# Spacing attention scans inside spectral blocks: 3.0 slots for the first eight, 2.035 for the other forty, and PSUM banks lent from slot 10

## The chip, the core and the metric

The kernel runs on one core of one Trainium2 chip. A core has a matrix engine (TensorE: PE in the profile, with its weight loads listed apart as PEld), a vector engine (VectorE, DVE), a scalar engine (ScalarE, ACT), GpSimd (POOL), and SyncE (SP), which here only issues DMA transfers. Each engine runs its own instructions in the order in which they were written into its queue, and waits on semaphores for the others. Matrix products land in PSUM, which the program uses as eight banks of 128 x 512 float32.

The metric is the device time of one execution in microseconds (us), the median of three runs. Lower is better.

## What is computed

Two token mixers over 2048 tokens of width 512, joined by a gate:

```python
def _A_ref(x, wqkv, wo):            # attention, H = 32 heads of Dh = 16
    qkv = (x @ wqkv).reshape(B, S, 3, H, Dh).transpose(2, 0, 3, 1, 4)
    q, k, v = qkv[0], qkv[1], qkv[2]
    scores = jnp.einsum("bhqd,bhkd->bhqk", q, k) * scale
    p = _softmax(scores, axis=-1)
    o = jnp.einsum("bhqk,bhkd->bhqd", p, v)
    return o.transpose(0, 2, 1, 3).reshape(B, S, D) @ wo

def _B_ref(x, dft_seq_re, dft_seq_im, dft_hid_re, dft_hid_im):
    a = jnp.einsum("bsd,ed->bse", x, dft_hid_re)
    b = jnp.einsum("bsd,ed->bse", x, dft_hid_im)
    return jnp.einsum("ts,bse->bte", dft_seq_re, a) - jnp.einsum("ts,bse->bte", dft_seq_im, b)

g = _sigmoid((x * gate_w).sum(-1, keepdims=True))
return g * a + (1 - g) * b          # a, b: what the two return
```

## The kernel before

The program has four stages: projections (queries, keys, values and the two hidden-axis DFT products), the spectral stage (the sequence-axis DFT products), attention proper, and a last stretch in which attention runs beside the rest of the spectral work and the output projection. Float32 operands are split into a high and a low part in the format float32r, and a product is made of three: high x high, high x low, low x high.

**Scans.** Softmax subtracts a row maximum. The maxima are found in advance by *scans*: scan `n` computes a 128 x 512 piece of scores for the two heads of a pair and reduces it. Of the 1024 scans, the first 708 (`FRONT`) are put between other work ahead of attention. From scan 64 on they are folded (`scan_folded`, L160 to L181). Scan `n` has two halves, `j` = 0 and 1, for the two heads; each is one matmul (L174) with 64 contraction rows in its own half of the array, into its own PSUM bank. For even `c` ScalarE copies the result out (L178, `Relu`, tile `fold`); for odd `c` VectorE adds the new result to that tile and takes a maximum into `mx` (L180, one custom instruction and a short read of its accumulator). So scans alternate: one whose two banks ScalarE empties, then one whose two banks VectorE empties. The second half of scan `n` is issued together with the first half of scan `n+1` (`behind`).

**Slots.** All the product loops ahead of attention call `beside()` (L328 to L356) after each pair of product matmuls (`halves_of`, L201 to L205: two matmuls, one per half of the array, in two banks). One such call is a *slot*; `slots[0]` counts them. At each slot `beside` first runs what has fallen due (`after(n, f)` puts work `n` slots ahead: copies, splits, DMA issues), then adds `1 / pace[0]` to a credit and issues a scan when the credit reaches 1. `pace[0]` is thus a distance in slots: `PACE` 3.9, `SUMS` 5.2 and `BESIDE` 2.72 in the projections, `PART` 2.15 in most of the spectral stage, `SWAP` 2.97 while operands are exchanged in its middle.

**Blocks.** The spectral stage makes 22 *blocks* of 48 slots: 16 output row blocks `t` of phase 0 (`cr`, the cosine part), six of phase 1 (`ci`, the sine part). A block accumulates 96 product matmuls into the two banks of one *side*; sides alternate from block to block (`turns`, `xy`). Two blocks in each phase are made in halves (14 and 15 in phase 0, 0 and 1 in phase 1): that is where the operands are exchanged and `SWAP` holds. When a block is done, ScalarE scales its two banks into SBUF: `tx` at once (L771), `ty` five slots later (through `after`, so it has the line L318). GpSimd adds the two and SyncE stores the sum.

**Banks.** Four of the eight banks belong to the two sides. The other four, `d0`, `d1`, `k0`, `k1`, are the two *beds* of the scans (a bed is a bank for each half). A finished side is idle until the block after the next needs it, so it is lent as a third bed, `w`. `spare` holds the side and the slots between which it may be lent:

```python
if 0 < t < NB - 3 and n < len(coef) - NU - 1:      # L774, at a block's end
    spare[:] = side_of[t], slots[0] + 12, slots[0] + 44
...
side, since, until = spare                         # L296, in bed()
free = ["d", "k"] + ["w"] * (since <= slots[0] < until)
at = min(free, key=lambda a: places.get(a, -3))    # least recently used
```

So of the 48 slots of a block that follows a block with `0 < t < 13`, the first eleven and the last five have two beds and the rest have three. That holds for the twelve blocks `t` = 2 to 13 of phase 0 and for the three blocks `t` = 2 to 4 of phase 1, the fifteen blocks that the change reaches.

Of the kernel before, what the change touches and what calls it, by code (L numbers as in the profile page):

```python
# [37 lines left out]
FRONT = 564 + 16 * LATER - SAVED  # L38
FOLDED = range(SCANS, FRONT)
PACE, SUMS, BESIDE, PART, SWAP = 3.9, 5.2, 2.72, 2.15, 2.97  # L40
EARLY = [0, 4, 5, 6, 7, 1, 2, 3, 8, 9]
PARTS = {10: 20, 11: FRONT - SCANS * len(EARLY) - 20}
PART_PAIR, END_PAIR = PARTS
SEQ = [(p, i) for p in EARLY for i in range(SCANS)]
SEQ += [(p, i) for p, n in PARTS.items() for i in range(n)]
SEQ += [(p, i) for p in (PART_PAIR, 12, 13, 14, 15, END_PAIR) for i in range(PARTS.get(p, 0), SCANS)]
ROWS = {SCANS * n + (20 if n else 40): p for n, p in enumerate(EARLY[1:])}
ROWS.update({SCANS * len(EARLY) - 60: PART_PAIR, SCANS * len(EARLY) - 34: END_PAIR})
NWARM = 20
# [17 lines left out]
def build(tc, xT, wqkv, wo, wrT, wiT, cr, ci, ct, gate, out):  # L67
    nc = tc.nc
    with ExitStack() as ctx:
# [76 lines left out]
        def scan(n, ps):  # L146

            p, i = SEQ[n]
            qb, c = i // 4, i % 4
            qs, ks = scanned[p]  # L150
            if i == 0:
                new_maxima(p)
            for j in range(2):
                b = 64 * j
                nc.tensor.matmul(ps[:, j, :], qs[b:b + 48, qb * P:(qb + 1) * P],  # L155
                                 ks[b:b + 48, c * 512:(c + 1) * 512], start=True, stop=True)
            nc.vector.tensor_reduce(mx[p][:, :, qb, c], ps, axis=AX.X, op=ALU.max)  # L157
# [3 lines left out]
        def scan_folded(n, j, bank, pool):  # L161

            p, i = SEQ[n]
            qb, c = i // 4, i % 4
            if i == 0 and j == 0:
                new_maxima(p)
                if p in PARTS:  # L170
                    nc.vector.memset(mx[p], -3.0e38)
            qs, ks = scanned[p]
            b, ps = 64 * j, bank(n, j)
            nc.tensor.matmul(ps, qs[b:b + 64, qb * P:(qb + 1) * P], ks[b:b + 64, c * 512:(c + 1) * 512],  # L174
                             start=True, stop=True)
            if c % 2 == 0:
                fold[j] = pool.tile([P, 512], F32, tag=f"fold{j}", name="fold")
                nc.scalar.activation(fold[j], ps, AF.Relu)  # L178
            else:
                nc.vector.tensor_tensor_reduce(out=fold[j], in0=ps, in1=fold[j], scale=1.0, scalar=-3.0e38,  # L180
                                               op0=ALU.add, op1=ALU.max, accum_out=mx[p][:, j, qb, c // 2:c // 2 + 1])  # L181

        def shift(p, copy=nc.vector.tensor_copy, sub=nc.vector.tensor_sub):
# [9 lines left out]

            of = mx[p].rearrange("p j b c -> p (j b) c")[:, :, 0:2 if p in EARLY[1:] else 4]
            return [lambda: nc.vector.tensor_reduce(m, of, axis=AX.X, op=ALU.max, negate=True),
# [73 lines left out]
        seen, slots, due, count = [0], [0], [], [0]  # L269
        pace = [None, 0.0]  # L270
        with ExitStack() as pf:

            def s1():
                return pss1[0].tile([P, 2, 512], F32, tag="s1", name="s1")
# [3 lines left out]
            spare = [0, 0, 0]  # L278
# [31 lines left out]
            def run_due(force=(False, False)):  # L310

                while True:
                    ready = [d for d in due if d[0] <= slots[0] or force[d[2] in maxima]]
                    if not ready:
                        return
                    d = min(ready, key=lambda d: d[:2])
                    due.remove(d)
                    d[2](*d[3])  # L318

            def load_scan_beside(p):  # L320
                scanned[p], loads = row_loads(p, nc.sync, kf_d if p else k_d, p > 0)
                for n, load in enumerate(loads):
                    after(7 * n, load)
# [4 lines left out]
            def beside():  # L328

                slots[0] += 1  # L330
                run_due()
                if pace[0] is None:
                    return
                pace[1] += 1.0 / pace[0]
                while seen[0] < FRONT and pace[1] >= 1.0:
                    pace[1] -= 1.0
                    n = seen[0]
                    if n == FOLDED.start:
                        begin_folds()
                    if n in ROWS:  # L340
                        load_scan_beside(ROWS[n])
                    if n not in FOLDED:
                        scan(n, s1())
                        done = n
                    else:

                        scan_folded(n, 0, *beds)
                        done = behind(n - 1)
                    seen[0] += 1
                    if seen[0] == FRONT:  # L350
                        done = behind(n)
                    if done is not None and SEQ[done][1] == SCANS - 1:
                        for d, part in enumerate(shift(SEQ[done][0], nc.scalar.copy, nc.gpsimd.tensor_sub)):
                            maxima.append(part)
                            after((3, 8, 26, 31, 36)[d], part)
# [59 lines left out]
            def begin_folds():  # L415

                banks.close()
                psk.append(ctx.enter_context(tc.tile_pool(name="psk", bufs=1, space=PSUM, side="right", reuse_waits="tile")))
                beds.extend((bed, fp))
                scan_at(BESIDE)  # L420
# [255 lines left out]
            with ExitStack() as py:  # L676
# [11 lines left out]
                pss, yre, early, side_of = {}, {}, {}, {}  # L688
# [24 lines left out]
                for n, (ph, t, u) in enumerate(coef):  # L713
# [49 lines left out]
                    if u == NU - 1:  # L763
                        tx = cp.tile([P, D], F32, tag="tx", name="tx")
                        last = n == len(coef) - 1
                        ty = cp.tile([P, D], F32, tag="raw" if last else "ty", name="ty", bufs=5 if last else 2)
                        if last:
                            for v, ps in zip((tx, ty), pss[t]):
                                nc.vector.tensor_scalar_mul(v, ps, gm[:, t:t + 1])
                        else:  # L770
                            nc.scalar.mul(tx, pss[t][0], gm[:, t:t + 1])  # L771
                            if n == len(coef) - NU - 1:
                                nc.scalar.mul(ty, pss[t][1], gm[:, t:t + 1])
                            else:  # L774
                                after(5, nc.scalar.mul, ty, pss[t][1], gm[:, t:t + 1])
                        after(10, mixed, ph, t, yre.get(t), tx, ty)
                        if 0 < t < NB - 3 and n < len(coef) - NU - 1:
                            spare[:] = side_of[t], slots[0] + 12, slots[0] + 44
                run_due((True, True))

        assert seen[0] == FRONT + 1 and turns[0] % 2 == SCANS_IN, (seen, turns)
# [580 lines left out]
```

## Time and profile before

| | |
|---|---|
| median of three runs | 1711.61 us (1710.64 to 1711.81) |
| profiled execution, its own time | 1711.22 us |
| its span, first to last instruction | 1709.4 us |
| granted TensorE clock, mean | 0.999 |
| projections | 0 to 296.8 us |
| spectral stage | 296.8 to 658 us |
| attention, then attention beside the rest | 658 to 1258, 1258 to 1709 us |

Busy time in a view counts an engine as busy from an instruction's start to its end, and matmuls are pipelined: two run in the two halves of the array at once, and the next is taken in before the last is out. TensorE therefore shows nearly no idle time even where it loses time, and a loss is seen in two other ways: as more time for the same number of matmuls, and as idle time of the weight loader (PEld) that ends when ScalarE or VectorE has emptied a bank. In views of windows, "(x38)" counts the instructions that touch the window, so those that lie across its edges are in the count of both neighbours.

### The profile page before, as it was taken

To read this page: it belongs to the slowest core of one execution; us is meant where nothing else is said; L and a number is where in the kernel's file an instruction comes from. 1 tells how busy PE (TensorE), PEld (TensorE's weight loads), DVE (VectorE), ACT (ScalarE), POOL (GpSimd) and SP (SyncE) were. 2 spreads that over 40 slices of the span, in tenths; PEclk is the share of its full clock that TensorE was granted. 3 is DMA by queue.
4 is the path that set the end of the run, shared out by engine and by line. 5 is a ranking of instruction groups with operands and counts; after the bars stand their busy time and mean duration, and the time that the engine had idled before them with its cause. 6 is when DMAs were issued, how large, how long until landed. Compare 5 with 4: busy or idle time off the path is not lost.

```text
span 1709.4 us, 36306 instructions
## 1 busy us (share of the span) xinstructions
PE 1697.7 (99%) x13560; PEld 1022.3 (60%) x13560; DVE 1187.3 (69%) x2179; ACT 1491.7 (87%) x2472; POOL 764.3 (45%) x909
## 2 busy tenths in 40 slices
PE   9999999999999999999999999999999999999998
PEld 6888889989888885333333333333345555555554
DVE  5898888899999996666666666666642455654343
ACT  5447889888888888999999999999998888889876
POOL 3673435755555761434544455353423333334222
PEclk9999999999999999999999999999999999999999
DMA  7784557534348764356444445353436465576733
GB/s 253 246 284 106 155 167 230 172 117 121 115 121 219 197 135 95 97 133 138 136 114 111 122 121 134 95 131 78 100 69 145 136 151 146 142 164 163 194 92 127
DMA packets 149665, 246.73 MB, mean 144 GB/s; under 512 B 50048, under 2 KB 60784, under 8 KB 142192
## 3 DMA queue, kind: packets, MB, share of 16 engines
q1 hardware_dynamic: 134224, 223.04, 47.7%
q0 software_dynamic: 14688, 20.33, 4.9%
q8 instruction: 106, 1.74, 0.5%
q10 hardware_dynamic: 576, 1.05, 0.2%
q14 instruction: 71, 0.58, 0.1%
HBM read 164.10 MB, written 81.01 MB: 143 GB/s over the span
## 4 chain that ended last, share of the span: by engine, by line
PE 97%; DMA 1%; DVE 0%; issue 0%; ACT 0%; SPq 0%; DVEq 0%; ACTq 0%
PE pvb L808 29%; PE xy L205 26%; PE s L230 19%; PE s L174 9%; PE s L205 9%; PE s L155 5%; DMA q_d<-eh 0%; DMA raws<-wqkv 0%; DMA raws<-xT 0%; PE s L597 0%; DVE y L923 0%; DVE fold L180 0%; ACT fold L178 0%; SPq L567 0%; SPq L566 0%
## 5 line engine op out<-in xcount | busy, mean ns | idle before, releaser
L254 ACT ACTIVATE eb<-s 128x1024 f32<-128x1024 f32 x512 | 579.7, 1132 | 59.5 <-PE s L230 59.5
L262 ACT ACTIVATE e<-s 128x512 f32<-128x512 f32 x1022 | 609.4, 709 | 0.0
L157 DVE TENSOR_REDUCE mx<-s 128x2 f32<-128x1024 f32 x380 | 461.0, 1225 | 196.5 <-PE s L155 196.3
L808 PE MATMUL pvb<-eb,va 128*17 128x512 f32 x2052 | 514.4, 597 | 0.0
L808 PE MATMUL pvb<-e,va 128*17 128x512 f32 x2044 | 513.6, 597 | 0.0
L180 DVE CUSTOM_DVE_ANT_0 fold<-s,fold 128x512 f32<-128x512 f32 x644 | 432.5, 690 | 54.8 <-PE s L174 28.0
L178 ACT ACTIVATE fold<-s 128x512 f32<-128x512 f32 x644 | 376.8, 603 | 78.7 <-PE s L174 60.3
L230 PEld LDWEIGHTS s<-qs,ks 50*128 50x128 f32 x2048 | 214.0, 184 | 361.6 <-ACT eb L254 269.4
L230 PE MATMUL s<-qs,ks 50*128 50x512 f32 x2048 | 424.0, 435 | 0.0
L205 PE MATMUL xy<-b,c 64*128 64x512 f32 x2448 | 388.7, 391 | 0.1
L174 PE MATMUL s<-ks,qs 64*128 64x512 f32 x1288 | 319.2, 401 | 1.6 <-DVE mx L180 0.9
L205 PEld LDWEIGHTS xy<-b,c 64*128 64x128 f32 x2448 | 283.3, 184 | 28.4 <-issue 1.0
L174 PEld LDWEIGHTS s<-ks,qs 64*128 64x128 f32 x1288 | 173.9, 184 | 36.3 <-DVE mx L180 10.8
L808 PEld LDWEIGHTS pvb<-eb,va 128*17 128x17 f32 x2052 | 69.8, 96 | 189.3 <-issue 180.0
L155 PE MATMUL s<-ks,qs 48*128 48x512 f32 x760 | 153.4, 394 | 0.0
L205 PE MATMUL s<-b,b 64*128 64x512 f32 x1050 | 136.4, 391 | 0.0
L827 POOL DMA_DIRECT2D r_d<-lc x31 | 18.0, 580 | 260.3 <-DVE lc L826 212.7
L820 POOL DMA_DIRECT2D lc<-ob x124 | 63.1, 515 | 117.2 <-DVE ob L817 112.0
L205 PE MATMUL xy<-w,b 64*128 64x512 f32 x768 | 115.4, 391 | 0.0
L205 PEld LDWEIGHTS s<-b,b 64*128 64x128 f32 x1050 | 100.2, 185 | 23.5 <-issue 1.0
L405 POOL TENSOR_TENSOR c<-craw,c 128x512 fp32r<-128x512 f32 x84 | 110.2, 1312 | 6.7
L829 POOL DMA_DIRECT2D rb<-r_d x124 | 60.5, 495 | 107.1 <-DMA r_d<-lc 101.3
(149 smaller groups left out, 1561.6 us busy)
## 6 DMA issues: line engine op xcount, KB each, us to landing
qs<-q_d SPq DMA_DIRECT2D x90, 256.0 KB
craw<-cr SPq DMA_DIRECT2D x60, 256.0 KB
craw<-ct SPq DMA_DIRECT2D x48, 256.0 KB
ks<-k_d SPq DMA_DIRECT2D x46, 256.0 KB
ks<-kf_d SPq DMA_DIRECT2D x44, 256.0 KB
kept_None<-sum SPq DMA_DIRECT2D x40, 256.0 KB
craw<-kept_None SPq DMA_DIRECT2D x40, 256.0 KB
craw<-ci SPq DMA_DIRECT2D x32, 256.0 KB
```

The costliest lines, as they stand in the source:

```text
L155: nc.tensor.matmul(ps[:, j, :], qs[b:b + 48, qb * P:(qb + 1) * P], ks[b:b + 48, c * 512:(c + 1) * 512], start=True, stop=True)
L157: nc.vector.tensor_reduce(mx[p][:, :, qb, c], ps, axis=AX.X, op=ALU.max)
L174: nc.tensor.matmul(ps, qs[b:b + 64, qb * P:(qb + 1) * P], ks[b:b + 64, c * 512:(c + 1) * 512], start=True, stop=True)
L178: nc.scalar.activation(fold[j], ps, AF.Relu)
L180: nc.vector.tensor_tensor_reduce(out=fold[j], in0=ps, in1=fold[j], scale=1.0, scalar=-3.0e38, op0=ALU.add, op1=ALU.max, accum_out=mx[p][:, ...
L205: nc.tensor.matmul(ps[j], lhs[r], rhs[r], start=first, stop=last)
L230: nc.tensor.matmul(pss[j], ks[b:b + 50, kb * P:(kb + 1) * P], qs[b:b + 50, q0:q0 + 512], start=True, stop=True)
L254: nc.scalar.activation(e, ps, AF.Exp, scale=SCALE)
L262: nc.scalar.activation(e[j], pss[j], AF.Exp, scale=SCALE)
L405: sub(lo, raw, hi.bitcast(F32))
L808: nc.tensor.matmul(pvb[r:r + VC, :], va[:, kb, 2 * p + j, :], es[c][j], start=kb == 0, stop=kb == NB - 1, tile_position=(0, r))
L820: nc.gpsimd.dma_start(lc[32 * n:32 * n + 32, :], ob[r + DH:r + VC, :].rearrange("p (s e) -> p s e", e=16))
```

## The change

A scan's distance in a block that follows a lending block is 3.0 slots in the block's first eight slots (`CALM`) and 2.035 in the other forty (`KEEN`), in place of 2.15 throughout; 8/3.0 + 40/2.035 = 22.32 scans per block, and 48/2.15 = 22.33 before. Outside those blocks, and wherever the pace is not `PART`, nothing is different: `since` counts the slots from the end of the last lending block, and is over 48 there. The idle side is lent from slot 10 of the block, before from slot 12.

```diff
 PACE, SUMS, BESIDE, PART, SWAP = 3.9, 5.2, 2.72, 2.15, 2.97
+CALM, KEEN = 3.0, 2.035
@@ beside()
                 if pace[0] is None:
                     return
-                pace[1] += 1.0 / pace[0]
+                since = slots[0] - spare[1] + 10
+                pace[1] += 1.0 / (pace[0] if pace[0] != PART or since > 48 else CALM if since <= 8 else KEEN)
@@ at a block's end
                         if 0 < t < NB - 3 and n < len(coef) - NU - 1:
-                            spare[:] = side_of[t], slots[0] + 12, slots[0] + 44
+                            spare[:] = side_of[t], slots[0] + 10, slots[0] + 44
```

On TensorE the start of block `t` = 10 of phase 0 shows it. L205 (L206 in the changed file, which is two lines longer) are the product matmuls, a slot each row; L174 (L175) are scan matmuls, the second half of one scan and the first half of the next. Before:

```order
L205 MATMUL xy<-b_4207,c 128x512 x2
L205 MATMUL xy<-b_4208,c 128x512 x2
L174 MATMUL s<-ks,qs 128x512 x2
L205 MATMUL xy<-b_4207,c 128x512 x2
L205 MATMUL xy<-b_4281,c 128x512 x2
L174 MATMUL s<-ks,qs 128x512 x2
L205 MATMUL xy<-b_4282,c 128x512 x2
L205 MATMUL xy<-b_4281,c 128x512 x2
L174 MATMUL s<-ks,qs 128x512 x2
L205 MATMUL xy<-b_4353,c 128x512 x2
L205 MATMUL xy<-b_4354,c 128x512 x2
L174 MATMUL s<-ks,qs 128x512 x2
```

And now:

```order
L206 MATMUL xy<-b_4207,c 128x512 x2
L206 MATMUL xy<-b_4208,c 128x512 x2
L175 MATMUL s<-ks,qs 128x512 x2
L206 MATMUL xy<-b_4207,c 128x512 x2
L206 MATMUL xy<-b_4281,c 128x512 x2
L206 MATMUL xy<-b_4282,c 128x512 x2
L175 MATMUL s<-ks,qs 128x512 x2
L206 MATMUL xy<-b_4281,c 128x512 x2
L206 MATMUL xy<-b_4353,c 128x512 x2
L206 MATMUL xy<-b_4354,c 128x512 x2
L175 MATMUL s<-ks,qs 128x512 x2
```

The first eight product rows had four scan rows among them and now have three. The one taken out is given back over the forty slots behind, where nearly every scan now stands two slots after the last.

On ScalarE the same place, from the end of block 9 to the end of block 10. `tx` and `ty` are the two copies of a finished block, `fold` the copies of scan halves. Before:

```order
L771 ACTIVATE tx<-xy,gm 128x512
L178 ACTIVATE fold<-s 128x512 x2
L318 ACTIVATE ty<-xy,gm 128x512
L178 ACTIVATE fold<-s 128x512 x20
L771 ACTIVATE tx<-xy,gm 128x512
```

And now:

```order
L773 ACTIVATE tx<-xy,gm 128x512
L179 ACTIVATE fold<-s 128x512
L319 ACTIVATE ty<-xy,gm 128x512
L179 ACTIVATE fold<-s 128x512 x21
L773 ACTIVATE tx<-xy,gm 128x512
```

One scan copy that stood ahead of `ty` stands behind it; the number of copies in a block is the same.

## The prediction

> **What bounds the kernel now.** I read the page first, then windows over the spectral stage, then the groups and waits of its undisturbed blocks, then one block's timeline.
>
> ```profile
> span 1709.4 us, 36306 instructions
> PE 97%; DMA 1%; DVE 0%; issue 0%; ACT 0%; SPq 0%; DVEq 0%; ACTq 0%
> ```
>
> TensorE is on the chain of waits nearly throughout, so a microsecond taken from its queue anywhere ahead of the end is a microsecond of the whole; and since its busy time hides losses, I look for stretches in which the same matmuls take longer. The fifteen blocks that the change reaches split at the first matmul of a lent bank (slot 11 or 12) into a front and a tail. Windows over the fronts, three of the fifteen rows and the sum; the columns are the window, then busy time and instructions of PE, PEld, DVE, ACT and POOL, then clock, DMA share and GB/s:
>
> ```profile
> 329.63:333.60 3.97, 3.97 (x38) 3.63 (x34) 3.46 (x13) 3.77 (x8) 3.10 (x3) 1.00 0.64 179
> 462.40:467.15 4.75, 4.75 (x40) 3.34 (x37) 4.31 (x13) 4.34 (x9) 3.21 (x3) 1.00 0.57 160
> 512.41:516.61 4.20, 4.20 (x39) 3.86 (x36) 3.68 (x13) 3.97 (x9) 3.10 (x3) 1.00 0.72 188
> sum 64.40, PE 64.40 PEld 53.87 DVE 56.82 ACT 60.75 POOL 47.33; mean PE 4.29 PEld 3.59 DVE 3.79 ACT 4.05 POOL 3.16
> ```
>
> And over the tails, three rows and the sum:
>
> ```profile
> 333.60:346.56 12.96, 12.95 (x111) 11.83 (x109) 11.61 (x35) 10.00 (x18) 6.11 (x8) 1.00 0.50 150
> 450.37:462.40 12.03, 12.03 (x107) 10.77 (x104) 10.87 (x34) 9.15 (x18) 5.99 (x7) 1.00 0.26 82
> 467.15:479.19 12.04, 12.04 (x106) 9.67 (x104) 11.19 (x33) 9.71 (x17) 5.73 (x6) 1.00 0.68 185
> sum 184.10, PE 184.09 PEld 164.41 DVE 169.68 ACT 145.81 POOL 91.44; mean PE 12.27 PEld 10.96 DVE 11.31 ACT 9.72 POOL 6.10
> ```
>
> The pace comes from the tails. The one from 450.37 holds 104 matmuls of the program (107 touch the window, three across its edges): 52 pairs in 12.03 us, 0.2313 us a pair. By the program's order the fifteen fronts hold 528 matmuls, 264 pairs, and the tails 1582, 791 pairs. At 0.2313 they would take 61.06 and 182.96 us. They take 64.40 and 184.10: **3.34 us are lost in the fronts and 1.14 us in the tails**, 4.5 us in all. The loss is uneven: the front from 462.40 has 36 matmuls, 4.16 us at that pace, and loses 0.59; that from 512.41 has as many and loses 0.04; the tail from 333.60 (108 matmuls, 12.49 us) holds 0.47 of the tails' 1.14.
>
> What the fronts wait for: the groups of blocks 2 to 13, what ended the idle time of the scans' weight loads there, and the timeline of block 10's front (start, duration, engine and line, count, then idle time ahead and its releaser).
>
> ```profile
> L180 DVE CUSTOM_DVE_ANT_0 fold<-s,fold 128x512 f32<-128x512 f32 x269 | 179.8, 690 | 17.7 <-PE s L174 6.8 <-ACT fold L178 3.5 <-PE xy L205 0.6
> L178 ACT ACTIVATE fold<-s 128x512 f32<-128x512 f32 x269 | 154.9, 602 | 33.6 <-PE s L174 25.7 <-DVE mx L180 0.5
> L318 ACT ACTIVATE ty<-xy,gm 128x512 f32<-128x512 f32 x12 | 8.5, 706 | 0.0
> L771 ACT ACTIVATE tx<-xy,gm 128x512 f32<-128x512 f32 x12 | 8.2, 683 | 0.0
> ```
>
> ```profile
> its engine sat idle before it (us, times) until:
>   ACT fold L178: 2.7, 8
>   DVE mx L180: 2.3, 11
> ```
>
> ```profile
> 463.91 1.09 ACT L178 ACTIVATE fold<-s 128x512 f32<-128x512 f32 x2
> 464.57 0.19 PEld L174 LDWEIGHTS s<-ks,qs 64*128 64x128 f32 x2 [0.33 <-ACT fold L178]
> 464.87 0.71 ACT L318 ACTIVATE ty<-xy,gm 128x512 f32<-128x512 f32 x1
> 465.30 0.19 PEld L174 LDWEIGHTS s<-ks,qs 64*128 64x128 f32 x2 [0.21 <-DVE mx L180]
> 465.44 1.12 ACT L178 ACTIVATE fold<-s 128x512 f32<-128x512 f32 x2
> 466.12 0.19 PEld L174 LDWEIGHTS s<-ks,qs 64*128 64x128 f32 x2 [0.29 <-ACT fold L178]
> ```
>
> Nineteen waits of the weight loader in twelve blocks, eight on ScalarE's copies and eleven on VectorE. At a block's end ScalarE gets `tx` and `ty`, 0.68 and 0.71 us, on top of its scan copies at 0.60. With two beds a scan may not start before the one two ahead of it has been emptied. So the scan at 464.57 waits for a copy that stood behind `tx`, that at 466.12 for one behind `ty`, and the VectorE scan between them for a fold that needed the late copy. ScalarE is busy for 60.75 us of the fronts, as much as they would take unhindered (61.06): **in the fronts ScalarE is the bound.** In the tails it is busy for 145.81 of 184.10 us (79%) and VectorE for 169.68 (92%).
>
> **The change part by part.** The reckoning goes against the profiled execution, 1711.22 us, 1.8 above its span; the median of the runs is 0.4 above that.
>
> *Sparser scans in the first eight slots.* A front of eleven and a half slots had 11.5/2.15 = 5.35 scans and now has 8/3.0 + 3.5/2.035 = 4.39, so 0.96 fewer. A scan costs ScalarE one copy on average (two for every other scan): 0.58 us less of its 4.05, which leaves 3.47. TensorE is relieved of 0.96 pairs, 0.22 us of the unhindered 4.07, which leaves 3.85. ScalarE falls from as much as the front lasts to 90% of it. A copy that stood ahead of `ty` in block 10 now stands behind, and a bed has three slots and a scan, eight pairs or 1.85 us over two scans, in which to be emptied, where it had 1.39 to 1.62. What stays: at the best all 3.34 us go; at the worst none, if the delay only moves to slot 9. The nearest rows are the fronts from 329.63 and 512.41, in which ScalarE was busy for 3.77 and 3.97 us and which lose 0.04 each (3.97 against 17 pairs, 4.20 against 18). At 3.47 us I take 0.05 per block: 15 x 0.05 = 0.75 stays, **-2.6 us**.
>
> *Lending from slot 10.* The third bed then comes a scan earlier, and what is left of the delay meets it. Its banks must have been scaled out. In block 10 the scan of the tenth slot went out at 466.12, `ty` had ended at 465.58, and the half whose bank `ty` reads goes out one scan after the other; so even with the front's 0.6 us gone nothing new waits. It is part of the -2.6 and no term of its own; were `ty` a microsecond later, it would cost one wait of the kind above, 0.3 us a block.
>
> *Denser scans in the other forty.* A scan and its slots are now 3.035 pairs or 0.702 us, before 3.15 pairs or 0.729. VectorE gets one fold per scan on average, and takes the next one 0.62 us after the last where they stand in a row:
>
> ```profile
> 462.26 0.69 DVE L180 CUSTOM_DVE_ANT_0 fold<-s,fold 128x512 f32<-128x512 f32 x1 [0.31 <-PE s L174]
> 462.88 0.69 DVE L180 CUSTOM_DVE_ANT_0 fold<-s,fold 128x512 f32<-128x512 f32 x1
> ```
>
> By 0.62 of 0.702 it is 88% taken; by its busy time, 92% x 0.729/0.702 = 96%. ScalarE goes from 79 to 82%. No row shows a tail at that pace. From below: nothing, or even a part of the tails' 1.14 regained, since 0.47 of it lies in one tail. From above: tails that lose as the fronts do, 5.5% of 183 us, +10 us. The nearest rows are the tails themselves, at 92% and 0.6% lost; those from 450.37 and 467.15 keep the pace to 0.01. I take **+0.3 us**.
>
> *Handing the bank back.* The last lent scan now ends nearer to the block that needs the bank: by the order at least 14 matmuls lie between (22 before), 14 or 16 at ten of the fifteen block starts. 14 are seven pairs, 1.62 us, for a matmul (0.39 us) and a fold (0.69): 0.54 to spare. If the engine has one more fold in hand (0.62), 0.08 us are missing. Between 0 and 10 x 0.1; I take **+0.1 us**, and what is late then is the block's first product, with everything behind it on TensorE.
>
> *Around them.* The exchange of operands keeps its pace; by the order a few scans there move by one slot. It is the stretch with the largest losses:
>
> ```profile
> 528.64:577.62 48.98, 48.02 (x396) 39.58 (x393) 45.30 (x120) 40.70 (x76) 34.05 (x33) 1.00 0.75 209
> ```
>
> Of its 48.98 us TensorE is even shown idle for 0.96. A moved scan could gain or lose one such wait, within 1 us either way; I take 0. The DMA issues tied to scan numbers (the rows of the next head pair) move by a slot or two, 0.3 to 0.7 us, on transfers that the program issues 24 or more scans ahead: nothing. Attention and all that follows are unchanged and start earlier or later by the sum.
>
> Sum: -2.6 + 0.3 + 0.1 = **-2.2 us**: 1709.0 for the profiled execution, and with the 0.4 to the median **1709.4 us**. That is 0.13% below 1711.61; some 0.2% (3.4 us) is what a measurement of this kernel tells from no change, so my forecast is "the same", on the fast side.
>
> **Rivals.**
>
> *All of it goes.* The tails' waits are of the same kind (a bed not emptied), and the earlier third bed and the even spacing remove them as well: -4.5, less some remainder, **1707.2 us**. For it: the order has most scans of a tail two slots apart on three beds, which is the rhythm of the tails that lose nothing. Against it: the last five slots still have two beds, at the densest pace.
>
> *The delay only moves.* ScalarE owes 1.39 us for `tx` and `ty` in every block, and at the denser pace pays it off more slowly (0.702 - 0.60 = 0.10 us a scan, before 0.13). If the waits come at slots 9 to 20 instead, nothing is won: **1711.5 us**. Against it: three beds let a scan be late by 0.7 us more.
>
> *VectorE becomes the bound of the tails.* Place: the forty dense slots. It decides once a fold takes more than 0.702 us of VectorE's time, from start to next start with all its gaps; its bare 0.69 leaves little, though the 0.62 in a row leaves enough. Then the beds fill, the loss is carried over the bank's return into the next front, and tails lose as ScalarE's fronts did: +10 - 2.6, **1719 us**. For it: 92% busy now. The Trainium skill, TensorEngine Tiling (Array Packing), section PSUM Bottleneck, speaks for this rival too: packing row tiles speeds the matrix engine but not the emptying of PSUM, which may become the bottleneck. The tails of this trace do not yet show that, at 0.6% lost; the fronts do.
>
> **How the numbers follow.** Forecast 45% (its own range 1708.0 to 1710.8, from 0.6 more regained in fronts and tails to 1.4 less), all of it 27%, only moved 13%, VectorE 15%. Faster by over 0.2% (below 1708.2): 27% and a tenth of the forecast's, 0.31. Slower by over 0.2% (above 1715.0): 0.15. Within: 0.54. The range runs from 1706.9, just below "all of it", to 1712.6, above "only moved" with an adverse microsecond in the exchange; outside lie the VectorE case and little else.
>
> **What would show it.** In the changed profile: the fronts' loss against 0.2313 us a pair falls from 3.34 to about 0.75 us and ScalarE's share of the fronts to about 90%; idle weight loads before L175 that end with ScalarE's copy become few; the tails keep their pace, VectorE at about 96% busy; the first products of blocks do not wait for a bank. The forecast is wrong if the tails lose more than 2 us, if waits appear at block starts, or if the fronts still lose over 2 us.

## The result, and the profile after

| | before | changed |
|---|---|---|
| median of 22 runs each, on the same chip | 1711.65 us (1710.64 to 1713.53) | 1708.42 us (1707.70 to 1709.66) |
| profiled execution | 1711.22 us, span 1709.4 | 1708.37 us, span 1706.6 |

The ratio is 0.9981, 95% interval 0.9975 to 0.9987: 3.2 us or 0.19% less, 1.0 us under the predicted 1709.4 and inside the forecast's own range (1708.0 to 1710.8). That is just within the 0.2% that the prediction calls "the same", though the interval is clear of 1.

The page of the changed kernel begins as that of before did, with TensorE on the chain almost throughout:

```profile
span 1706.6 us, 36271 instructions
PE 98%; DVE 0%; ACT 0%; DMA 0%; issue 0%; SPq 0%; DVEq 0%
```

To lay two kernels side by side I cut every block at the same place, the first product of its thirteenth slot: twelve slots are the front, thirty-six the tail. (The prediction cut at the first lent bank, which the change moves.) So cut, the fronts of before, as a view of windows with the columns explained in the prediction, sum to this, for 522 matmuls (261 pairs, 60.37 us at 0.2313 us a pair):

```profile
sum 63.69, PE 63.69 PEld 53.25 DVE 56.13 ACT 60.32 POOL 47.01; mean PE 4.25 PEld 3.55 DVE 3.74 ACT 4.02 POOL 3.13
```

And of the changed kernel, the fronts of blocks 10 and 2 and the sum of all fifteen (496 matmuls, 57.36 us):

```profile
460.38:464.10 3.72, 3.72 (x34) 3.71 (x33) 3.10 (x10) 3.27 (x7) 3.04 (x3) 1.00 0.40 127
329.33:333.30 3.97, 3.97 (x37) 3.88 (x35) 3.10 (x11) 3.77 (x7) 3.02 (x3) 1.00 0.64 187
...
sum 57.85, PE 57.85 PEld 52.27 DVE 47.70 ACT 54.32 POOL 46.43; mean PE 3.86 PEld 3.48 DVE 3.18 ACT 3.62 POOL 3.10
```

The fronts lost 3.33 us and now lose 0.48 (57.85 against 57.36, rounded sums). Block 10's front, the worst before, has 32 matmuls (34 touch the window) in 3.72 us, 0.02 over sixteen pairs. The tails of the changed kernel, the same two blocks and the sum (1614 matmuls, 186.66 us):

```profile
447.85:460.38 12.53, 12.53 (x111) 12.32 (x108) 11.70 (x38) 10.77 (x19) 6.06 (x8) 1.00 0.28 90
333.30:346.14 12.84, 12.83 (x111) 12.36 (x109) 11.97 (x37) 10.85 (x19) 6.13 (x8) 1.00 0.54 151
...
sum 187.55, PE 187.54 PEld 171.94 DVE 180.02 ACT 159.82 POOL 92.16; mean PE 12.50 PEld 11.46 DVE 12.00 ACT 10.65 POOL 6.14
```

VectorE is busy for 180.02 of 187.55 us, 96%, and the tails lose 0.90 us, before 1.14. (The first of these rows is block 9's tail, just ahead of block 10's front.)

In blocks 2 to 13 the waits of the scans' weight loads before had two releasers, ScalarE eight times (2.7 us) and VectorE eleven times (2.3 us). After, the same view of line L175 has one:

```profile
its engine sat idle before it (us, times) until:
  DVE mx L181: 1.3, 6
```

By their times, fourteen of the nineteen waits before lay in fronts, all eight of ScalarE's among them. The other five, all on VectorE, lay in slots 45 to 48 of the tails, where two beds stand. Of the six waits after, five lie in those last slots and one in the first slot of a block.

The timeline of block 10's front shows why (start, duration, engine and line, operation, count; a wait would stand at the row's end):

```profile
461.14 0.68 ACT L773 ACTIVATE tx<-xy,gm 128x512 f32<-128x512 f32 x1
...
461.54 0.26 PEld L175 LDWEIGHTS s<-ks,qs 64*128 64x128 f32 x2
461.70 0.60 ACT L179 ACTIVATE fold<-s 128x512 f32<-128x512 f32 x1
...
462.18 0.70 ACT L319 ACTIVATE ty<-xy,gm 128x512 f32<-128x512 f32 x1
...
462.48 0.26 PEld L175 LDWEIGHTS s<-ks,qs 64*128 64x128 f32 x2
462.75 1.11 ACT L179 ACTIVATE fold<-s 128x512 f32<-128x512 f32 x2
...
463.40 0.26 PEld L175 LDWEIGHTS s<-ks,qs 64*128 64x128 f32 x2
```

Scans now come 0.92 to 0.94 us apart, and none waits. ScalarE still runs late behind `ty` (the copy at 462.75 starts when the next scan's weights are already in), but the bank it empties first is asked for again only at 463.40.

Where the 2.8 us of span went, stage by stage. A loss is time over 0.2313 us a pair; the exchange is blocks 14 to 17; the last row is what is left after block 21's own loss.

| us | before | after | difference |
|---|---|---|---|
| start of the spectral stage (untouched projections) | 296.77 | 296.48 | -0.29 |
| loss in the fifteen fronts | 3.33 | 0.48 | -2.85 |
| loss in the fifteen tails | 1.14 | 0.90 | -0.24 |
| loss in blocks 0 and 1 | 1.18 | 1.16 | -0.02 |
| loss in the exchange | 4.13 | 4.10 | -0.03 |
| loss in the last block, 21 | 0.76 | 1.21 | +0.45 |
| the rest, to the end of the span | | | +0.2 |

The fronts carry the gain. The last block, which no term of the prediction held, gave 0.45 back.

### The profile page after: what moved, and what is told of

Its sections match the earlier page's. It is cut to its first block, busy times and chain, and to the rows that moved or that the text cites. A ratio compares the mean times of both kernels' runs of the same rounds, so it can differ in the third digit from the quotient of the medians.

```text
span 1706.6 us, 36271 instructions
## 1 busy us (share of the span) xinstructions
PE 1694.6 (99%) x13560; PEld 1032.2 (60%) x13560; DVE 1188.1 (70%) x2179; ACT 1499.3 (88%) x2472; POOL 764.4 (45%) x909
## 3 DMA queue, kind: packets, MB, share of 16 engines
q10 hardware_dynamic: 576, 1.05, 0.2%
## 4 chain that ended last, share of the span: by engine, by line
PE 98%; DVE 0%; ACT 0%; DMA 0%; issue 0%; SPq 0%; DVEq 0%
PE pvb L810 29%; PE xy L206 26%; PE s L231 19%; PE s L175 9%; PE s L206 9%; PE s L156 5%; DMA raws<-wqkv 0%; PE s L599 0%; ACT fold L179 0%; DVE y L925 0%; DVE fold L181 0%; SPq L569 0%; SPq L568 0%; ACT ty L319 0%; PE s L1312 0%
## 5 line engine op out<-in xcount | busy, mean ns | idle before, releaser
L179 ACT ACTIVATE fold<-s 128x512 f32<-128x512 f32 x644 | 383.9, 602 | 68.4 <-PE s L175 38.3
L206 PE MATMUL xy<-b,c 64*128 64x512 f32 x2448 | 383.4, 390 | 0.2 <-ACT c L375 0.2
L175 PE MATMUL s<-ks,qs 64*128 64x512 f32 x1288 | 291.9, 398 | 2.1 <-DVE mx L181 1.2
L206 PEld LDWEIGHTS xy<-b,c 64*128 64x128 f32 x2448 | 269.4, 184 | 25.4 <-issue 1.0
L175 PEld LDWEIGHTS s<-ks,qs 64*128 64x128 f32 x1288 | 153.6, 184 | 29.1 <-DVE mx L181 10.6
L156 PE MATMUL s<-ks,qs 48*128 48x512 f32 x760 | 157.9, 394 | 0.0
L206 PE MATMUL s<-b,b 64*128 64x512 f32 x1050 | 136.5, 391 | 0.0
L206 PE MATMUL xy<-w,b 64*128 64x512 f32 x768 | 115.3, 391 | 0.0
L206 PEld LDWEIGHTS s<-b,b 64*128 64x128 f32 x1050 | 100.3, 185 | 23.5 <-issue 1.0
L406 POOL CAST c<-craw 128x512 fp32r<-128x512 f32 x84 | 52.4, 624 | 117.1 <-PE xy L206 116.3
```

Source lines behind the costliest of these rows:

```text
L206: nc.tensor.matmul(ps[j], lhs[r], rhs[r], start=first, stop=last)
```

## The experiments

The theory: in the fronts scans come faster than ScalarE, which also has `tx` and `ty` to do, can empty two beds; sparser scans cure that, and a third bed carries the rest. The rivals: the lending from slot 10 alone does it; VectorE becomes the bound once scans are dense; the handed-back bank is late.

Besides medians, the table gives for each profiled run the losses of the stages, and the span less the start of the spectral stage. The last leaves out the projections, which no kernel here changes and whose end moved between 296.1 and 299.0 us from one profile to the next. The losses are of one profile each; the same kernel, profiled twice (changed and e12), differs by 0.30 in the tails and by 0.1 at most in the other columns of loss. In e5 no scans are left for block 21, and pairs of products alone are faster than 0.2313 us (36 of them took 8.16 us in block 20, 0.227 each), so its loss there comes out below zero.

| kernel | median us | ratio to before (95%) | fronts | tails | block 1 | exchange | block 21 | span less start |
|---|---|---|---|---|---|---|---|---|
| before | 1711.65 | 1 | 3.33 | 1.14 | 0.38 | 4.13 | 0.76 | 1412.6 |
| changed | 1708.42 | 0.9981 (0.9975 to 0.9987) | 0.48 | 0.90 | 0.38 | 4.10 | 1.21 | 1410.1 |
| e1_pace_only | 1709.76 | 0.9989 (0.9980 to 0.9998) | 0.93 | 1.57 | 0.38 | 4.15 | 0.93 | 1411.2 |
| e2_lend_only | 1711.33 | 0.9998 (0.9989 to 1.0007) | 3.30 | 0.97 | 0.37 | 4.08 | 0.50 | 1412.6 |
| e3_no_ty | 1709.12 | 0.9985 (0.9977 to 0.9994) | 1.53 | 0.92 | 0.23 | 3.88 | 0.77 | 1410.6 |
| e4_calm_last | 1708.62 | 0.9980 (0.9971 to 0.9989) | 0.42 | 0.52 | 0.37 | 4.08 | 0.76 | 1409.1 |
| e5_keen18 | 1716.36 | 1.0031 (1.0019 to 1.0044) | 1.01 | 2.41 | 0.36 | 10.59 | -0.14 | 1422.3 |
| e7_until47 | 1712.42 | 1.0008 (0.9999 to 1.0017) | 2.90 | 2.09 | 0.39 | 4.11 | 1.38 | 1413.9 |
| e8_edges | 1706.65 | 0.9972 (0.9962 to 0.9983) | 0.46 | 0.49 | 0.17 | 3.64 | 0.49 | 1408.3 |
| e9_edges_swap | 1707.57 | 0.9977 (0.9968 to 0.9987) | 0.38 | 1.05 | 0.12 | 2.61 | 0.77 | 1408.9 |
| e10_no_copies | one run, 1706.94 | | 0.78 | 0.76 | 0.12 | 3.53 | 0.77 | 1408.9 |
| e11_edges_swap2 | 1707.94 | 0.9979 (0.9970 to 0.9988) | 0.67 | 0.18 | 0.16 | 3.55 | 0.89 | 1408.5 |
| e12_changed_again | 1708.64 | 0.9984 (0.9975 to 0.9993) | 0.39 | 0.60 | 0.38 | 4.10 | 1.20 | 1409.7 |

### The spacing alone: e1_pace_only

```diff
-                since = slots[0] - spare[1] + 10
+                since = slots[0] - spare[1] + 12
-                            spare[:] = side_of[t], slots[0] + 10, slots[0] + 44
+                            spare[:] = side_of[t], slots[0] + 12, slots[0] + 44
```

> The change's spacing (3.0 slots for the first eight, 2.035 after) with the idle side still lent from slot 12. Theory, ScalarE's debt after a block's end (two copies of 0.7 us) decides and the sparser scans let it be paid: the fronts of the fifteen blocks lose under 1 us where before lost 3.3, and the time is 2 to 3 us under before. Rival, the earlier third bed is what removes the waits: the fronts still lose over 2 us, waits at slots 9 to 11, time within 1 us of before.

Measured: ratio 0.9989 (0.9980 to 0.9998), 1.7 us below before in the same series (1711.44). Sum of its fronts, 496 matmuls:

```profile
sum 58.32, PE 58.32 PEld 53.69 DVE 47.52 ACT 54.15 POOL 46.24; mean PE 3.89 PEld 3.58 DVE 3.17 ACT 3.61 POOL 3.08
```

They lose 0.93 us, under 1 as the theory had it, so the spacing alone takes 2.40 of the 2.85; the time falls a little short of its 2 to 3 us. But the tails lose 1.57, more than in either kernel. Part of that is the late return of the lent bank. Which bed a scan gets goes by turns, so the slot from which the side is lent also moves the last lent scan. Counted in the program's order as in the prediction, only 10 or 12 matmuls lie between that scan and the block that needs the bank at seven block starts (14 at least in the changed kernel, 22 before). In blocks 2 to 13 three first products of a block wait for it, 0.7 us in all.

### The lending alone: e2_lend_only

```diff
# to the kernel before
-                            spare[:] = side_of[t], slots[0] + 12, slots[0] + 44
+                            spare[:] = side_of[t], slots[0] + 10, slots[0] + 44
```

> Scans 2.15 slots apart throughout as before, the idle side lent from slot 10. Theory (the spacing decides): most waits of the fronts lie ahead of slot 10 and stay, the fronts lose 2 to 3 us, the time is 0.3 to 1.2 us under before. Rival (the third bed decides): the fronts lose under 1 us and the time is over 2 us under before.

Measured: ratio 0.9998 (0.9989 to 1.0007). The sum of its fronts, 522 matmuls, is that of before to 0.03 us:

```profile
sum 63.66, PE 63.44 PEld 54.17 DVE 55.37 ACT 60.17 POOL 46.61; mean PE 4.23 PEld 3.61 DVE 3.69 ACT 4.01 POOL 3.11
```

That misses the theory's 2 to 3 us, and the rival's under 1 by far. But the sum hides that the waits are other ones. Of the product loads (L205) of blocks 2 to 13, none waited before. Here:

```profile
its engine sat idle before it (us, times) until:
  DVE mx L180: 1.8, 5
  ACT fold L178: 0.6, 3
```

Seven of the eight are weight loads, 2.3 us together, at the starts of blocks 4, 5, 7, 8, 10, 11 and 13 (the eighth is the matmul behind the load of block 10). At these seven only 8 or 10 matmuls lie between the last lent scan and the block's first product; at blocks 3, 6, 9 and 12, which do not wait, it is 14, and before the change 22 at least. The scans' own waits in these blocks fall from nineteen (5.0 us) to seven (1.9). Slot by slot, blocks 2 to 13 lose 1.33 us in slots 1 to 4, before 0.37, and 1.76 in slots 5 to 12, before 2.61. So lending alone gains no time, but not because the third bed does nothing: its earlier start brought a late return with it. How much the bed saves by itself is not shown, since a block that starts late also gives ScalarE time to catch up.

With the sparse spacing, lending from slot 10 goes with 0.45 us less in the fronts (0.93 to 0.48) and 0.67 in the tails (1.57 to 0.90). e1 runs the ninth to eleventh slot at the dense spacing on two beds, the changed kernel only the ninth; but 0.37 of the 0.45 lies in the fronts of blocks 5, 8, 11 and 12, which begin with four of e1's seven late returns, and 0.43 of the 0.67 in the tail of block 20, at whose end the weight loader waits 0.51 us ahead of another. Most of what lending from slot 10 adds, then, goes by where the last lent scan falls.

### One of ScalarE's two copies out: e3_no_ty, and both: e10_no_copies

```diff
# e3_no_ty, to the kernel before
-                                after(5, nc.scalar.mul, ty, pss[t][1], gm[:, t:t + 1])
+                                ty = tx
# e10_no_copies: as e3, and
-                            nc.scalar.mul(tx, pss[t][0], gm[:, t:t + 1])
+                                nc.gpsimd.memset(tx, 0.0)
```

> The kernel before without ScalarE's second copy ty of a block (the first copy tx is added to itself in its place, so the spectral part of the output is left wrong for most row blocks); 0.7 us less of ScalarE per block, scans and banks as before. Theory, ScalarE is the bound of the fronts: the fronts lose under 0.8 us (before 3.3), and the time is 2.5 us or more under before. Rival, two beds are too few at 2.15 slots whatever ScalarE does: the fronts still lose over 2 us and the time is within 1.5 us of before.

> The kernel before without both of ScalarE's copies at a block's end (tx is set to zero by GpSimd and used for ty too, so the spectral part of the output is left out for nearly all row blocks). Without ty alone the fronts lost 1.5 us of 3.3. Theory A, all of the fronts' loss is ScalarE's two copies: now under 0.4 us. Theory B, two beds at 2.15 slots fall short by themselves as soon as a scan is late for any reason: 1 us or more stays.

Measured: the sums of the fronts, first of e3, then of e10, both with 522 matmuls (60.37 us) at the old even spacing:

```profile
sum 61.89, PE 61.89 PEld 54.27 DVE 56.38 ACT 54.75 POOL 46.03; mean PE 4.13 PEld 3.62 DVE 3.76 ACT 3.65 POOL 3.07
```

```profile
sum 61.17, PE 61.17 PEld 56.61 DVE 56.30 ACT 49.27 POOL 45.84; mean PE 4.08 PEld 3.77 DVE 3.75 ACT 3.28 POOL 3.06
```

The fronts' loss falls from 3.33 to 1.53 us without `ty` and to 0.78 us without both; both fall between the two sides that had been set. So ScalarE's two copies make 2.55 of the 3.33 us. Of the 0.78 that stays, two beds at 2.15 slots can account for a part at most: no weight load of e10's fronts waits over 0.15 us, and eleven of the fifteen lose 0.01 to 0.05, which the changed kernel's do as well (0.01 to 0.08). Its share is a coarse guide, too: e3 keeps it busy for 3.65 us a front and loses 1.53, the changed kernel for 3.62 and loses 0.48. What differs is the spacing: 522 matmuls against 496 in the same slots.

### Much denser tails: e5_keen18

```diff
-CALM, KEEN = 3.0, 2.035
+CALM, KEEN = 3.0, 1.8
```

> The changed kernel with 1.8 slots between scans in the forty dense slots (the scans are then done before the last blocks, so the twelve blocks 2 to 13 are compared). A scan and its slots are 2.8 pairs, 0.648 us. Rival from the prediction (VectorE becomes the bound, by its busy time of 0.66 us per scan in the tails before): the tails of blocks 2 to 13 lose all along, 0.4 us or more each, over 5 us together. Theory (VectorE takes a fold 0.62 us after the last, so it still keeps up while three beds are there; what is short is the two beds of the last five slots): these tails lose 2 to 4 us together, in the last five slots and at block starts, and next to nothing in slots 13 to 43.

Measured: ratio 1.0031 (1.0019 to 1.0044). The tails lose 2.41 us, not 10. Those of blocks 2 to 13, which the expectation speaks of, lose 2.5, within the theory's 2 to 4. Their weight loads wait at the ends: 2.1 us in slots 45 to 48, where the third bed has been handed back, 1.2 in the first two slots, 0.2 at slot 11, and no wait over 0.15 between slots 12 and 44, which lose 0.05 to 0.09 us a block. At a spacing of 2.8 pairs or 0.648 us VectorE still follows where three beds stand. The rival falls; the waits lie where two beds stand.

The run is slower for another reason, which neither side had named: the exchange lost 10.59 us. The waits there, and then the row of the chain:

```profile
ACT b L749 <- DMA abr<-b_d: 6.5, 1, 6.5
...
PEld s L175 <- ACT fold L179: 6.0, 1, 6.0
```

```profile
572.57 9.98 DMA abr<-b_d
```

One copy of an operand on ScalarE (L749) waited 6.5 us for a transfer that took 9.98 us; the scan copies are queued behind it on ScalarE, and TensorE's next scan waited 6.0 us for them. The profiled execution (1720.55 us) is the longest of five, the median 4.2 us below it, so how much of this every run has stays open.

### The bank handed back at the last moment: e7_until47

```diff
-                            spare[:] = side_of[t], slots[0] + 10, slots[0] + 44
+                            spare[:] = side_of[t], slots[0] + 10, slots[0] + 47
```

> The changed kernel with the idle side lent until slot 47, not 44. By the order four block starts then have only 2 matmuls between the last lent scan and the first product on its bank, and four have 8; the others keep 14 or more. Theory (a bank is back a matmul, 0.39 us, and a fold, 0.69, after its scan's start, so from 10 matmuls down the product waits): 0.9 to 1.5 us at each of the four starts with 2, up to 0.5 at those with 8, together 4 to 7 us of loss at block starts, less the half microsecond of waits in the last slots that goes; the time is 3 to 6 us above the changed kernel. Rival (the return costs nothing, the two beds of the last slots are what costs): no waits at block starts, the time up to 0.9 us under the changed kernel.

Measured: median 1712.42 against the changed kernel's 1708.42, 4.0 us more, with ratios 1.0008 (0.9999 to 1.0017) and 0.9981 (0.9975 to 0.9987). The start of block 3 on the timeline:

```profile
346.51 0.52 PEld L206 LDWEIGHTS xy<-b,c 64*128 64x128 f32 x5 [0.66 <-ACT fold L179]
346.51 0.73 PE L206 MATMUL xy<-b,c 64*128 64x512 f32 x4 [0.35 <-ACT fold L179]
```

The first products of the block wait for a scan copy out of the bank that they need. Four block starts do so (blocks 3, 6, 9 and 20, whose fronts lose 0.70, 0.55, 0.59 and 0.56 us), and the fronts lose 2.90 in all. They are the four with only 2 matmuls in between; the banks with 8 are the other halves of the same four sides. (Block 7's front loses 0.29, but nothing there waits for a bank.) Ahead of each of the four the weight loader stands idle too, 0.3 to 0.7 us, which is in the tails' 2.09. So the hazard that the prediction priced exists, and slot 44 keeps clear of it: in the changed kernel those four fronts lose 0.02 each.

### The last block: e4_calm_last

The last block follows block 20, which lends nothing on, so it runs at 2.15 on two beds behind a tail that is now denser. Of the changed kernel, its rows:

```profile
641.65 0.69 ACT L775 ACTIVATE ty<-xy,gm 128x512 f32<-128x512 f32 x1
...
642.22 1.09 ACT L179 ACTIVATE fold<-s 128x512 f32<-128x512 f32 x2
...
642.88 0.19 PEld L175 LDWEIGHTS s<-ks,qs 64*128 64x128 f32 x2 [0.93 <-ACT fold L179]
```

One scan waits 0.93 us behind `ty`, the wait of the old fronts; the longest of that kind at the same place before was this:

```profile
646.08 0.19 PEld L174 LDWEIGHTS s<-ks,qs 64*128 64x128 f32 x2 [0.70 <-ACT fold L178]
```

The experiment gives the last block the sparse and the dense spacing, without lending:

```diff
+                        if n == len(coef) - NU - 1:
+                            spare[:] = 0, slots[0] + 10, slots[0]
```

> The changed kernel, with the sparse first eight slots in the last block of the spectral stage too (then 2.035 slots; no bank lent there). In the changed kernel's profile the scan at slot 5 of that block waits 0.66 us longer than unhindered, and there is another wait of 0.4 at slot 16. Theory: the same debt (tx and ty back to back at the end of the block before), so the sparse start removes the wait at slot 5 and the time is 0.5 to 1.2 us under the changed kernel. Rival: in a block without a lent bank the denser rest brings the wait back a few slots later, and the time is within 0.3 us of the changed kernel.

Measured: the block's loss falls from 1.21 to 0.76, its first twelve slots' from 0.83 to 0.37. The ratio, 0.9980 (0.9971 to 0.9989), can't tell that from the changed kernel, and the medians are within the rival's 0.3 us, so the gain is shown in the block's loss alone.

### Sparse starts everywhere: e8_edges

Here every block's first eight slots are sparse, block 1 and the last among them, and the dense spacing holds only where a bank is lent.

```diff
-            spare = [0, 0, 0]
+            spare, edge = [0, 0, 0], [-48]
-                since = slots[0] - spare[1] + 10
-                pace[1] += 1.0 / (pace[0] if pace[0] != PART or since > 48 else CALM if since <= 8 else KEEN)
+                since, lent = slots[0] - edge[0], spare[1] == edge[0] + 10
+                pace[1] += 1.0 / (pace[0] if pace[0] != PART else CALM if since <= 8 else KEEN if lent and since <= 48 else PART)
@@ at a block's end
+                        edge[0] = slots[0]
```

> The changed kernel with the sparse first eight slots after every block's end at this pace, also in the blocks in which nothing is lent (1 and the last, and the first whole one of phase 1); there the pace goes back to 2.15 afterwards. Theory (ScalarE's two copies at a block's end are what the scans run into): block 1 loses 0.1 to 0.2 us less, the last block 0.5 to 0.9 less, the time is 0.5 to 1.2 us under the changed kernel. Rival (with two beds the waits only move): within 0.3 us of the changed kernel.

Measured: 1706.65 us, ratio 0.9972 (0.9962 to 0.9983), the lowest median of all. Block 1 loses 0.17 in place of 0.38, the last block 0.49 in place of 1.21. Its rows there hold no wait:

```profile
640.79 0.69 ACT L775 ACTIVATE ty<-xy,gm 128x512 f32<-128x512 f32 x1
640.92 0.22 PEld L175 LDWEIGHTS s<-ks,qs 64*128 64x128 f32 x2
...
641.86 0.35 PEld L175 LDWEIGHTS s<-ks,qs 64*128 64x128 f32 x2
...
642.55 0.39 PEld L175 LDWEIGHTS s<-ks,qs 64*128 64x128 f32 x2
```

It beats the kernel before. Against the changed kernel the intervals overlap (0.9962 to 0.9983, 0.9975 to 0.9987); by the profiles it is 1.4 to 1.8 us shorter from the start of the spectral stage on (1408.3 against 1409.7 and 1410.1). That is more than the theory's 0.5 to 1.2: besides the two blocks, 0.46 us comes from the exchange (3.64 for 4.10), which was in no sum. Block 1's gain shows again in e9 (0.12) and e11 (0.16); the last block's doesn't (0.77 and 0.89), so it may hang on which scan happens to meet `ty`, which no run tried.

### A sparser exchange: e9_edges_swap and e11_edges_swap2

```diff
# e9, to e8: 3.3 wherever SWAP holds
-PACE, SUMS, BESIDE, PART, SWAP = 3.9, 5.2, 2.72, 2.15, 2.97
-CALM, KEEN = 3.0, 2.035
+PACE, SUMS, BESIDE, PART, SWAP = 3.9, 5.2, 2.72, 2.15, 3.3
+CALM, KEEN = 3.0, 2.0
# e11, to e8: 3.3 in the exchange alone
-CALM, KEEN = 3.0, 2.035
+CALM, KEEN = 3.0, 2.02
-                        scan_at(SWAP)
+                        scan_at(3.3)
```

> As the run before, and the scans that are 2.97 slots apart during the exchange of operands 3.3 apart, with 2.0 in place of 2.035 in the dense slots to make up. In the changed kernel's profile blocks 14 to 17 lose 4.1 us against 0.2313 us a pair, with ScalarE and VectorE copying operands between the folds. Theory (the exchange's losses are the same debt, so fewer scans there help): blocks 14 to 17 lose 2 to 3 us, the dense slots no more than before, the time is 1.5 to 3 us under the changed kernel. Rival (these waits come from single long instructions, VectorE's subtractions of 1.4 to 1.6 us beside GpSimd's, which a scan runs into whatever the spacing): blocks 14 to 17 still lose over 3.5 us.

> The sparse first eight slots after every block's end, 3.3 slots during the exchange of operands only (not at the stage's start), 2.02 in the dense slots. Blocks 14 to 17 lose 2.5 to 3.2 us (4.1 in the changed kernel), the tails no more than 0.9, block 0 stays at 0.8; the time is 2 to 3 us under the changed kernel and at or under that of the run with the edges alone. If the single long instructions of the exchange decide, it is within 0.5 us of that run.

Measured: in e9 the exchange loses 2.61 us in place of 3.64, but block 0 loses 1.07 in place of 0.79, the tails 1.05 in place of 0.49, the last block 0.77 in place of 0.49. What the sparser stretch gains, the places that must take its scans give back (ratio 0.9977, 0.9968 to 0.9987). In e11 the exchange loses 3.55, hardly less than e8's 3.64, at the same 3.3 (ratio 0.9979, 0.9970 to 0.9988). So it was not the 3.3 as such that gained in e9; that the scans fall on other slots there was not tried by itself. Both miss the times that were expected: e9 is 0.9 us under the changed kernel by the medians, not 1.5 to 3, and e11 0.5 under and 1.3 above e8. Neither beats e8.

### The changed kernel again: e12_changed_again

No edit.

> The changed kernel once more, on the same chip and in the same rounds as the run before, for the comparison: 2.5 to 4 us under the kernel before, its fronts losing about 0.5 us and its last block about 1.2.

Measured: median 1708.64, ratio 0.9984 (0.9975 to 0.9993). Its profiled execution, 1710.43 us, is the longest of its eleven, and 2.5 us of that lie ahead of the spectral stage, which starts at 299.00. From there on it is within 0.4 us of the first profile, and the fronts (0.39), the exchange (4.10) and the last block (1.20) repeat to 0.1. The tails do not quite: 0.60 and 0.90.

## Why the prediction was right, and where it was off

**The bound of the fronts** held. "In the fronts ScalarE is the bound" is true of 2.55 of 3.33 us (e10); the 0.78 that stays without its two copies holds no wait over 0.15 us. But five of the nineteen waits that the prediction lists for the fronts lie in the tails' last slots, and these the change did not touch.

**Sparser scans, -2.6 us:** -2.85. The term was argued as 0.05 a block that stays, 0.75; 0.48 and 0.39 stayed. The cause is shown from two sides: the spacing alone gains 2.40 (e1), and without `tx` and `ty` the old spacing gains 2.55 (e10). ScalarE's busy time fell from 99.9% of the unhindered fronts (60.32 of 60.37) to 95% (54.32 of 57.36), not to 90%: 0.40 us a front less, where 0.58 had been reckoned. That the waits went all the same suggests that the distance between scans did more than ScalarE's share.

**Lending from slot 10, no term of its own:** right in the sum, since by itself it gains no time (e2). The account, that the third bed meets what is left of the delay, is not what the runs show: of the 0.45 us by which e1's fronts lose more, 0.37 lies in blocks that begin with a late return of the bank. That the slot of lending also sets where the last lent scan falls was not foreseen.

**Denser tails, +0.3 us:** this is the mis-sized term, and it has the wrong sign. The tails lost 0.24 us less in one profile of the changed kernel and 0.54 less in the other. VectorE came to 96% busy, as forecast, and cost nothing where three beds stand: every wait of the tails, before and after, lies in slots 45 to 48. The pitch of 0.62 us in a row, not the duration of 0.69, is what a fold takes, and there were 0.08 us to spare to 0.702. The +10 us case is refuted twice, here and at 0.648 us a scan in e5. The Trainium skill's TensorEngine Tiling (Array Packing), section PSUM Bottleneck, warns that emptying PSUM may become the bottleneck once tiling has sped up the matrix engine; this trace agrees in the old fronts, where ScalarE was that (60.32 of 60.37 us), and not in the tails at 96% of VectorE.

**Handing back, +0.1 us:** nothing to be seen; the fronts at whose starts it would show lose 0.01 to 0.08 each. So 14 matmuls are enough. e7 shows the mechanism with 2, 0.55 to 0.70 us at four starts, and e2 with 8 and 10, waits of 0.2 to 0.6 us at seven.

**Around them, 0:** the exchange went from 4.13 to 4.10. Not foreseen was the last block's +0.45, in both profiles: no line of the change mentions it. The block ahead of it now ends at the dense spacing, which may be why; e4, with a sparse start there, takes the 0.45 back.

**The sum.** For the profiled execution 1709.0 was forecast and 1708.37 measured, 0.6 less: fronts -0.25, tails -0.54, hand-back -0.1, start of the stage -0.3, blocks 0 and 1 and the exchange -0.05, last block +0.45, the rest +0.2. "All of it goes" (1707.2) came half true, since the tails' waits thinned a little as well; "the delay only moves" is refuted by tails that lose no more than before.

## What to carry to other kernels

- Where work is woven evenly into another stream, look at its loss per place in the period, not at the mean: one engine's extra duty (here two copies of 0.7 us) at a fixed place made most of the waits, and moving one woven item out of that place cost nothing where a third bed stood.
- A buffer that is lent must also come back: lending two slots earlier shifted the turns, and so the last lent scan, and the wait turned up at the return (e2, e1). Count the distance at both ends.
- A spacing rule that changes by block has borders; look at the first block past it.

## What the runs showed of the hardware

- **A longer wait costs more than its length.** In block 10's front before, a scan pair that had waited went in at 464.57 and the next products at 464.90, 0.33 us later; after, with no wait, the two lie at 461.77 and 462.01, 0.24 apart. (Each row counts the matmuls that run on from it.) The extra 0.1 us came behind the longer waits alone: in blocks 2 to 13 before, the next products come 0.33 to 0.34 us later after waits of 0.29 us and more, 0.23 to 0.27 after waits of 0.17 to 0.21, and 0.23 in the median without one.

```profile
464.57 0.50 PE L174 MATMUL s<-ks,qs 64*128 64x512 f32 x2
...
464.90 0.63 PE L205 MATMUL xy<-b,c 64*128 64x512 f32 x4
```

```profile
461.77 0.47 PE L175 MATMUL s<-ks,qs 64*128 64x512 f32 x2
...
462.01 0.93 PE L206 MATMUL xy<-b,c 64*128 64x512 f32 x6
```

- **VectorE's subtraction takes twice its time beside GpSimd's.** In the exchange of the changed kernel, the groups of 536 to 575 us show the same operation at two means, and the timeline the overlap:

```profile
L319 DVE TENSOR_TENSOR b<-early,b 128x512 fp32r<-128x512 f32 x6 | 7.0, 1170 | 0.0
L319 DVE TENSOR_TENSOR b<-abr,b 128x512 fp32r<-128x512 f32 x6 | 4.5, 743 | 0.0
```

```profile
547.12 1.30 POOL L407 TENSOR_TENSOR c<-craw,c 128x512 fp32r<-128x512 f32 x1
...
547.59 1.37 DVE L319 TENSOR_TENSOR b<-early,b 128x512 fp32r<-128x512 f32 x1
...
549.63 0.19 PEld L175 LDWEIGHTS s<-ks,qs 64*128 64x128 f32 x2 [0.68 <-DVE mx L181]
```

```profile
555.91 0.68 DVE L319 TENSOR_TENSOR b<-abr,b 128x512 fp32r<-128x512 f32 x1
555.92 1.81 POOL L407 TENSOR_TENSOR c<-craw,c 128x512 fp32r<-128x512 f32 x1
```

The subtraction of 547.59 starts inside GpSimd's and takes 1.37 us. The one of 555.91 starts just ahead and takes 0.68, and there it is GpSimd's that is longer, 1.81 us for 1.30. Behind the long subtraction a scan waits 0.68 us on VectorE. The Trainium skill, SBUF — State Buffer, section SBUF: two separate sides, says that a VectorE operation with two SBUF inputs and a GpSimd one exclude each other on a shared pair of ports for a whole instruction; the trace agrees, as the subtraction ends 0.54 us after GpSimd's, about as if it had begun then. That this makes a part of the exchange's 4.1 us is argued only; no run kept the two apart.
